# A decoding kernel on one core: TensorE tasks of one column width kept together

## The chip, the core and the metric

The kernel runs on one core of a Trainium2 chip. The core has a matrix engine (TensorE, PE in the profile; its weight loads are PEld), three engines for elementwise work (VectorE or DVE, ScalarE or ACT, GpSimd or POOL) and SyncE (SP), which starts the transfers from main memory. Each engine runs its own instructions in the order in which they were written, and waits on semaphores for the others. TensorE's results go to PSUM, eight banks of 128 partitions by 512 words; everything else lies in SBUF.

TensorE is 128 columns wide. A matmul whose stationary operand has 32 columns or fewer can be placed on one quarter of the array (`tile_position`), one with 64 on one half; up to four or two such matmuls over different columns can then be in the array together. In this text a task is 1-wide, 2-wide or 4-wide when its matmuls use 128, 64 or 32 columns.

The metric is the device time of one execution in microseconds.

## The reference

Eight sequences (B) each decode one token, with x of 448 elements. Two rounds of an attention layer and a dense layer, both with a layer norm in front and the input added behind:

```python
x = x + A(layernorm(x)); x = x + B(layernorm(x)); x = x + A(layernorm(x)); x = x + B(layernorm(x))

def A(x):                        # 16 query heads, 8 key/value heads, head size 256
    q = x @ wq                   # 448 -> 4096
    k, v = the last 1024 positions of the caches, each head used by two query heads
    p = softmax(q k^T / 16)
    return (p v) @ wo            # 4096 -> 448

def B(x):
    return silu(x @ w1) @ w2     # 448 -> 1792 -> 448
```

Both attention layers read the same caches: per sequence eight key and eight value blocks of 512 KB each, 8.4 MB. All is bfloat16, sums are float32.

## The kernel before

**Tiling.** 448 is three chunks of 128 and one of 64, and this last chunk makes for special cases all over the kernel. The weights wq, wo, w1 and w2 stay in SBUF; keys and values pass through 28 slots of 512 KB. A slot is loaded again when its last reader is done, in the fixed order K(0), V(0), K(1), V(1), and so on; SyncE issues these transfers in that order. Keys are transposed within their slot on VectorE (`KT`, L973), sixteen transposes a sequence.

**Stages of a sequence b.** `layer1(b)`: scores of layer 1 (L656, 4-wide) against the transposed keys; softmax (`softmax`, L666 to L702: maximum on VectorE, exponentials on ScalarE, 64-wide transposes of the probabilities at L685, the sum at L696); values (`pv_rows`, 4-wide L715, and `pv_cols`, 1-wide L741); the output projection wo, partly as rows (`rows_part`, 4-wide, L758, into bank XB) and for the last four blocks as columns (`cols_part`, L764, into bank YB). `fold` copies the rows to SBUF (`rowb`, L775) and adds them to the columns with four matmuls (L776). `layer2(b)` then starts with `chain(b)`: `up` evacuates x (`xb_evac`, L784), computes its statistics (`stat`, L789 to L793, then ScalarE and a Newton iteration), multiplies by w1 (L542), and makes hT from tanh (L819), `zh` (L820) and their product (L822); then w2 as rows (8 blocks) and columns (6 blocks, L764), `fold`, `xb_evac` again, the centred copy `xc` (L832 to L836) that ScalarE spreads into `xn`, the second wq (L854), and with it scores, softmax and values of layer 2.

In `cols_part` the four output chunks of a block follow one another: three of 128 columns and the last, 64 wide:

```python
bank[YB][0:(P if o < 3 else 64), o * XW:(o + 1) * XW], lhs(o, i)[:, 0:(P if o < 3 else 64)],
```

**Order of the work.** Sequences don't depend on each other, so layer 1 of the next one runs among layer 2 of this one. No loop sets this order: `add` collects tasks with the tiles that they read and write, and `Plan.schedule` (L79) plays the kernel through with estimated durations. A task's rank is the longest chain of estimated durations behind it. At each step the engine that is free first takes, among the tasks that are ready within 0.2 us, the one of highest rank; where that one isn't ready yet, a task that fits ahead of it. The result is one fixed order per engine; `emit` adds the semaphores.

**Zero matmuls.** Where TensorE would be idle in this plan, `schedule` puts in matmuls of 256 columns with a zero stationary operand (L1020), 128 wide, which add nothing to the bank that they write. It counts the columns streamed in the last 3.41 us and adds zero matmuls while the count is under 4500. A task's `shape` holds the columns that each of its matmuls streams and the number of matmuls that run side by side (1, 2 or 4); the estimated duration comes from it too. Before the change the second number is used for that and for nothing else, and the transposes of the probabilities, 64 wide, carry a 1.

## Time and profile before

| | |
|---|---|
| median of 3 timed runs | 299.21 us (298.16 to 305.74) |
| the profiled execution | 295.94 us, its span 294.2 us |
| mean granted TensorE clock | 0.930 |
| busy: TensorE, its weight loads, VectorE, ScalarE, GpSimd | 83%, 55%, 52%, 25%, 8% |
| transfers | 78.40 MB, mean 267 GB/s over the span |
| chain that ended last | PE 75%, DVE 10%, ACT 6%, DMA 4%, issue 3% |

The span runs from the first to the last instruction of the profiled execution. Busy time of TensorE is the union of its matmuls' times; they are pipelined, so a row such as "1.22 PE L764 ... x16" spans sixteen overlapping matmuls, and the start of the next row tells better how long they kept the engine. A row of grouped instructions reads: line, engine, operation, tile written and tiles read, shape (rows*columns of the stationary operand, then the moving one), count | busy us, mean ns of one | idle us of the engine before them and what ended it. The granted clock is the share of TensorE's full clock that the chip allowed.

### The profile page before, as it was taken

What the parts mean: (1) busy time and instruction counts of PE and PEld (TensorE: products, weight loads), DVE (VectorE), ACT (ScalarE), POOL (GpSimd) and SP (SyncE); (2) the same over time, 40 slices, a digit from 0 to 9 for tenths busy, and PEclk for the clock granted to TensorE, in tenths of its full rate; (3) what the DMA queues carried; (4) which work ended last, traced back from release to release, by engine and by line L of the source; (5) the groups of instructions that cost most, each with busy time, mean ns of one, the idle gap of its engine ahead of it and who ended that gap; (6) DMA issues with size and microseconds to landing.
All of it is one profiled execution on the core that took longest, in us unless ns stands there. A gap on an engine that the chain in (4) does not pass through costs nothing.

```text
span 294.2 us, 11387 instructions
## 1 busy us (share of the span) xinstructions
PE 244.7 (83%) x5159; PEld 161.7 (55%) x5159; DVE 152.7 (52%) x444; ACT 73.0 (25%) x234; POOL 22.7 (8%) x116
## 2 busy tenths in 40 slices
PE   1155659997989889969997999699969997999996
PEld 0142335754566557645664576456635664676863
DVE  7197101379165828660777186536662756122351
ACT  2022301201422062232222422422132221231221
POOL 6000000020002000200020002000200020002000
PEclk9999997989997999995999799989797979997998
DMA  7999999999595598868886987799569876100000
GB/s 266 358 416 406 400 388 347 415 407 410 222 344 219 179 392 285 295 228 345 281 299 214 359 290 287 285 358 316 192 223 370 296 264 218 72 2 4 3 4 1
DMA packets 30880, 78.40 MB, mean 267 GB/s; under 512 B 2272, under 2 KB 5296, under 8 KB 30448
## 3 DMA queue, kind: packets, MB, share of 16 engines
q1 hardware_dynamic: 30832, 77.68, 71.4%
q8 instruction: 40, 0.66, 0.8%
q14 instruction: 8, 0.07, 0.1%
HBM read 77.67 MB, written 0.01 MB: 264 GB/s over the span
## 4 chain that ended last, share of the span: by engine, by line
PE 75%; DVE 10%; ACT 6%; DMA 4%; issue 3%; SPq 1%; ACTq 0%
PE bank L715 14%; PE bank L656 11%; PE bank L1020 8%; PE bank L764 8%; PE bank L542 7%; PE bank L854 7%; PE bank L758 7%; DVE slot L973 6%; DMA slot<-in_A_k_cache_dram 4%; ACT qbd L640 3%; PE bank L685 3%; ACT e_sb L679 2%; PE bank L865 2%; PE bank L696 2%; PE bank L741 1%
## 5 line engine op out<-in xcount | busy, mean ns | idle before, releaser
L973 DVE STREAM_TRANSPOSE slot<-slot 128x512 uint32<-128x512 uint32 x128 | 83.0, 684 | 6.5 <-DMA slot<-in_A_k_cache_dram 6.2
L656 PE MATMUL bank<-slot,qbd 128*8 128x256 bf16 x1024 | 40.3, 292 | 11.7 <-DVE mseg L662 9.8
L715 PE MATMUL bank<-slot,pT_sb 128*2 128x256 bf16 x960 | 43.7, 312 | 0.4 <-ACT pT_sb L693 0.4
L1020 PE MATMUL bank<-wq_sb,cols_b 128*128 128x256 bf16 x218 | 39.0, 292 | 0.3 <-issue 0.3
L656 PEld LDWEIGHTS bank<-slot,qbd 128*8 128x8 bf16 x1024 | 23.2, 87 | 20.3 <-DVE mseg L662 12.8
L715 PEld LDWEIGHTS bank<-slot,pT_sb 128*2 128x2 bf16 x960 | 22.1, 91 | 9.4 <-issue 1.0
L640 ACT ACTIVATE qbd<-q1s 32x128 bf16<-32x128 bf16 x32 | 10.0, 313 | 60.9 <-PE bank L656 60.3
L701 DVE RECIPROCAL rl_sb<-bank 128x16 f32<-128x16 f32 x16 | 4.1, 258 | 40.0 <-PE bank L696 39.7
L1020 PEld LDWEIGHTS bank<-wq_sb,cols_b 128*128 128x128 bf16 x218 | 19.3, 101 | 9.8 <-issue 7.1
L854 PE MATMUL bank<-wq_sb,xn 128*4 128x256 bf16 (+1 forms) x384 | 23.0, 375 | 0.2 <-DVE qT L859 0.2
L726 DVE TENSOR_TENSOR oT<-bank,rl_sb 128x16 bf16<-128x16 f32 (+1 forms) x32 | 6.2, 195 | 32.3 <-PE bank L722 32.2
L720 ACT ACTIVATE o_sb<-bank 128x256 bf16<-128x256 f32 x32 | 12.2, 383 | 34.2 <-PE bank L715 18.7
L820 POOL TENSOR_SCALAR zh<-vt,rstd 128x14 f32<-128x14 f32 x9 | 3.1, 347 | 214.6 <-DVE rstd L561 150.0
L685 PE MATMUL bank<-ident,e_sb 128*64 128x16 bf16 x256 | 9.8, 185 | 11.7 <-ACT e_sb L679 11.4
L758 PE MATMUL bank<-w2o,oT 128*1 128x448 bf16 x256 | 16.8, 376 | 3.1 <-issue 3.1
L859 DVE STREAM_TRANSPOSE qT<-bank 128x256 f32<-128x256 f32 (+1 forms) x24 | 12.1, 525 | 13.1 <-PE bank L854 12.9
L542 PE MATMUL bank<-xbt,w_sb 128*128 128x32 bf16 x504 | 16.0, 177 | 1.7 <-issue 1.4
L685 PEld LDWEIGHTS bank<-ident,e_sb 128*64 128x64 bf16 x256 | 6.9, 116 | 17.8 <-ACT e_sb L679 15.2
L542 PEld LDWEIGHTS bank<-xbt,w_sb 128*128 128x128 bf16 x504 | 14.1, 97 | 3.3 <-issue 1.6
L775 ACT ACTIVATE rowb<-bank 128x448 bf16<-128x448 f32 x17 | 9.2, 543 | 26.6 <-PE bank L758 26.5
L662 DVE TENSOR_REDUCE mseg<-bank 128x1 f32<-128x256 f32 x32 | 12.8, 410 | 5.1 <-PE bank L656 4.8
L764 PE MATMUL bank<-hT,w2o 128*128 128x16 bf16 x192 | 14.7, 180 | 0.6 <-issue 0.6
(161 smaller groups left out, 277.6 us busy)
## 6 DMA issues: line engine op xcount, KB each, us to landing
slot<-in_A_k_cache_dram SPq DMA_DIRECT2D x64, 512.0 KB, 8.0
slot<-in_A_v_cache_dram SPq DMA_DIRECT2D x64, 512.0 KB, 6.1
w2o<-in_A_wo_dram SPq DMA_DIRECT2D x2, 1792.0 KB, 16.1
wq_sb<-in_A_wq_dram SPq DMA_DIRECT2D x3, 1024.0 KB, 6.8
w2o<-in_B_w_dram SPq DMA_DIRECT2D x1, 1568.0 KB, 14.7
w_sb<-in_B_w_dram SPq DMA_DIRECT2D x3, 448.0 KB, 12.0
wq_sb<-in_A_wq_dram SPq DMA_DIRECT2D x2, 256.0 KB, 10.0
w_sb<-in_B_w_dram SPq DMA_DIRECT2D x1, 128.0 KB, 11.7
```

Of the source, the lines that this page charges most:

```text
L542: fns.append(lambda e, o=o, i=i, c0=c0: e.matmul(bank[bank_i][:, c0:c0 + n], lhs(o, i), rhs(o, i).broadcast_to([P, n]) if wide else rhs(o, i),
L640: act(lambda e, q=q: e.activation(qbd[0][32 * q:32 * q + 32].rearrange("p k c (q r) -> p (k c) q r", r=2)[:, :, q, :], q1s[32 * t:32 * t + ...
L656: fns.append(lambda e, cb=cb, par=par, j=j, kvh=kvh, kv=kv: e.matmul(bank[sc][32 * j:32 * j + 8, k2 * 256:(k2 + 1) * 256], qbd[layer][:, k ...
L662: dve(lambda e: e.tensor_reduce(mseg[layer][:, k2:k2 + 1], bank[sc][:, k2 * 256:(k2 + 1) * 256], AX.X, ALU.max, negate=True), bk(sc), [("m ...
L685: pe([lambda e, uh=uh, ql=ql, k2=k2: e.matmul(bank[lb][64 * ql:64 * ql + 64, (k2 * 4 + uh) * 16:(k2 * 4 + uh) * 16 + 16], e_sb[ei][:, k2, ...
L715: fns.append(lambda e, qh=qh, uh=uh, j=j, vv=vv: e.matmul(bank[ob][32 * j:32 * j + 2, c0:c0 + DH], p_col(ei, k2, j, qh, uh), vv, start=(qh ...
L720: act(lambda e: e.activation(o_sb[oi][:], bank[ob][:, c0:c0 + DH], ACTF.Copy), bk(ob), [("o", oi)], 0.385, "oevh" if ob == OB[0] else "oev ...
L758: pe([lambda e, i=i, c=c: e.matmul(bank[XB][32 * c:32 * c + 1, 0:D], rhs(i), w_sb[:, i * D:(i + 1) * D], start=(first and i - i0 < 4), sto ...
L764: pe([lambda e, i=i, o=o: e.matmul(bank[YB][0:(P if o < 3 else 64), o * XW:(o + 1) * XW], lhs(o, i)[:, 0:(P if o < 3 else 64)], rhs(i).bro ...
L854: fns.append(lambda e, j=j, c=c, wb=wb, off=off, h0=h0, n=n, k2=k2: e.matmul(bank[wb][32 * j:32 * j + 4, h0:h0 + n], xn[:, part(c, k2), j, :],
L973: dve(lambda e, v=v: e.transpose(v, v), [("slot", s)], [("slot", s)], 0.67, "KT")
L1020: fill = (lambda e: e.matmul(bank[OB[0]][:, DH:2 * DH], zero_b.broadcast_to([P, P]), wq_sb[:, 0:DH], start=False, stop=True, skip_group_ch ...
```

## The change

Six things change together:

- `cols_part` makes its fourth output chunk 128 wide, like the others. The upper 64 partitions of that chunk then hold products with columns that belong to the next block of the weights. So `xb_evac` takes two copies instead of one: the first three chunks as before, and the fourth with a scale per partition (`mask4`) that is zero in the upper half. The centred copy `xc` is five 1-wide matmuls of 64 columns instead of nine, and ScalarE spreads it into `xn` with three copies instead of two, none of which reads another's result.
- The planner knows a current width (`mode`). A TensorE task of another width starts 0.1 us later (`SWITCH`), and a ready task of the current width gets 0.3 added to its rank (`stay`). Only tasks of the current width are put ahead of one that isn't ready.
- Zero matmuls take the width of the task that follows: one of 128 columns, or two of 64, or four of 32, each 256 streamed columns, planned as 0.107 us in each case. The transposes of the probabilities now count as 2-wide.
- In `up` the statistics go to bank YB and w1 to bank XB, the other way round than before, and w1 is five tasks that go through the inputs chunk by chunk instead of four that go through the outputs. `stat` and `xc` tell the planner their streamed columns (16 and 64 instead of 1 and 4).
- `zh` moves from GpSimd to VectorE. The small transposed maxima `mT` get a tile for each layer.
- Some estimated durations change (second exponential, `va`, `qT`).

```diff
-            best = max(soon, key=lambda t: t.rank)
+            key = (lambda t: t.rank + (stay if t.shape[1] == mode else 0.0)) if e == "pe" else (lambda t: t.rank)
+            best = max(soon, key=key)
...
-                fits = [t for t in soon if ready[t.idx] <= now and now + t.dur <= ready[best.idx] + 0.03]
+                fits = [t for t in soon if ready[t.idx] <= now and now + t.dur <= ready[best.idx] + 0.03
+                        and (e != "pe" or t.shape[1] == mode)]
...
-            best.start = max(free[e], ready[best.idx])
+            best.start = max(free[e] + (SWITCH if e == "pe" and best.shape[1] != mode else 0.0), ready[best.idx])
...
-                        t = Task("pe", [fn], dur, 0.0, "fill")
-                        t.shape = (cols, 1)
+                        t = Task("pe", fns, dur, 0.0, "fill")
+                        t.shape = (cols, best.shape[1])
...
-               [("e", ei, k2), "ident"], bk(lb), (16, 1), "pT%d" % layer)
+               [("e", ei, k2), "ident"], bk(lb), (16, 2), "pT%d" % layer)
...
-            bank[YB][0:(P if o < 3 else 64), o * XW:(o + 1) * XW], lhs(o, i)[:, 0:(P if o < 3 else 64)],
-            rhs(i).broadcast_to([P, XW]), start=False, stop=True, skip_group_check=True)
-            for i in ins for o in range(KC)], reads, bk(YB), (XW, 1), name)
+            bank[YB][:, o * XW:(o + 1) * XW], lhs(o, i), rhs(i).broadcast_to([P, XW]), start=False, stop=True,
+            skip_group_check=True) for i in ins for o in range(KC)], reads, bk(YB), (XW, 1), name)
...
-        act(lambda e: e.activation(xbt[:, 0:KC], xcols(), ACTF.Copy), bk(YB), ["xbt"], 0.18, "xbt")
+        act(lambda e: e.activation(xbt[:, 0:3], xcols()[:, 0:3], ACTF.Copy), bk(YB), [("xbt", 0)], 0.175, "xbt")
+        act(lambda e: e.activation(xbt[:, 3:4], xcols()[:, 3:4], ACTF.Copy, scale=mask4[:, 3:4]), bk(YB) + MASK4,
+            [("xbt", 1)], 0.175, "xbt")
...
-        stat(XB, 0, 4.0, 0)
-        for o0, o1 in ((0, 4), (4, 8), (8, 11), (11, 14)):
-            pe(proj(YB, C_W1 + o0 * CW, range(o0, o1), range(KC), w1_l,
+        stat(YB, C_S1, 4.0, 0)
+        for i, o0, o1 in ((0, 0, FC), (1, 0, FC), (2, 0, FC), (3, 0, 8), (3, 8, FC)):
+            k = i if o0 == 0 else KC
+            pe([lambda e, i=i, k=k, o=o: e.matmul(
+                bank[XB][:, C_W1 + o * CW:C_W1 + o * CW + CW], w1_l(o, i), xbt[:, k:k + 1].broadcast_to([P, CW]),
...
-        pool(lambda e: e.tensor_scalar(zh[:], vt[:], rstds[0][:, 0:1], None, op0=ALU.mult), ["vt", ("rstd", 0)],
-             ["zh"], 0.22, "zh")
+        dve(lambda e: e.tensor_scalar(zh[:], vt[:], rstds[0][:, 0:1], None, op0=ALU.mult), ["vt", ("rstd", 0)],
+            ["zh"], 0.234, "zh")
...
-           [lambda e, c=c: e.matmul(xc[:, 0:3 * XW], ones_b[:], xbt[:, c:c + 1].broadcast_to([P, 3 * XW]),
-                                    start=False, stop=(c == KC - 1), skip_group_check=True) for c in range(KC)] +
-           [lambda e, c=c: e.matmul(xc[0:64, 3 * XW:], ones_b[:, 0:64], xbt[:, c:c + 1].broadcast_to([P, XW]),
+           [lambda e, c=c: e.matmul(xc, ones_b[:], xbt[:, c:c + 1].broadcast_to([P, KC * XW]),
...
-        act(lambda e: e.activation(xd[:, 0:KC], xc[:, 0:KC * XW:XW].unsqueeze(2).broadcast_to([P, KC, 4]), ACTF.Copy,
-                                   scale=-1.0 / D), bk(XB), ["xn"], 0.19, "xn")
-        act(lambda e: e.activation(xd[64:128, 4], xd[0:64, 3], ACTF.Copy), ["xn"], ["xn4"], 0.2, "x4")
+        xv = xc[:, 0:KC * XW:XW].unsqueeze(2).broadcast_to([P, KC, 4])
+        act(lambda e: e.activation(xd[:, 0:3], xv[:, 0:3], ACTF.Copy, scale=-1.0 / D), bk(XB), [("xn", 0)], 0.21, "xn")
+        act(lambda e: e.activation(xd[0:64, 3], xv[0:64, 3], ACTF.Copy, scale=-1.0 / D), bk(XB), [("xn", 1)], 0.19, "xn")
+        act(lambda e: e.activation(xd[64:128, 4], xv[0:64, 3], ACTF.Copy, scale=-1.0 / D), bk(XB), [("xn", 2)], 0.19,
+            "xn")
...
+    fills = {n: [lambda e, j=j, m=P // n: e.matmul(
+        bank[OB[0]][m * j:m * j + m, DH:2 * DH], zero_b.broadcast_to([P, m]), wq_sb[:, 0:DH], start=False, stop=True,
+        skip_group_check=True, **({"tile_position": (0, m * j)} if m < P else {})) for j in range(n)] for n in (1, 2, 4)}
+    fill = (fills, 0.107, DH,
```

## The prediction, made before the change was run

> **What bounds the kernel now.** I read the page from the top, then the chain of work that ended last, then one period of the loop in the timeline.

> ```profile
> span 294.2 us, 11387 instructions
> PE 244.7 (83%) x5159; PEld 161.7 (55%) x5159; DVE 152.7 (52%) x444; ACT 73.0 (25%) x234; POOL 22.7 (8%) x116
> ...
> DMA  7999999999595598868886987799569876100000
> ...
> PE 75%; DVE 10%; ACT 6%; DMA 4%; issue 3%; SPq 1%; ACTq 0%
> ```

> The last row, the chain's shares by engine, says that the end is set by TensorE for three quarters of the time; the other engines appear on it with 10% or less. So a nanosecond of TensorE time counts if it lies on that chain, and not otherwise. The DMA row (tenths, 40 slices of 7.4 us) is full only in the slices from 7 to 74 us, where the weights and the first two batches are loaded. The chain, in order of time, has these pieces in one period of the loop:

> ```profile
> 228.88 1.08 PE bank L764 x16
> ...
> 235.23 1.75 PE bank L764 x24
> ```

> L764 is `cols_part`: 16 matmuls for wo and 24 for w2. All of them stand on the chain. Now the same kind of work in the timeline, one period earlier; the first number is the start, so the distance between two rows is what a group occupied:

> ```profile
> 170.86 1.22 PE L764 MATMUL bank<-oT,w2o 128*128 128x16 bf16 x16
> 172.01 0.61 PE L715 MATMUL bank<-slot,pT_sb 128*2 128x256 bf16 x16
> 172.55 0.57 PE L542 MATMUL bank<-xbt,w_sb 128*128 128x32 bf16 x16
> 172.97 0.24 PE L789 MATMUL bank<-xbt,ones_b 128*128 128x16 bf16 x4
> ...
> 174.81 0.71 PE L1020 MATMUL bank<-wq_sb,cols_b 128*128 128x256 bf16 x5
> 175.35 0.20 PE L722 MATMUL bank<-ident,o_sb 128*128 128x8 bf16 x2
> ...
> 176.53 1.82 PE L764 MATMUL bank<-hT,w2o 128*128 128x16 bf16 x24
> 178.28 0.21 PE L722 MATMUL bank<-ident,o_sb 128*128 128x8 bf16 x2
> ```

> Sixteen w1 matmuls, all 128 columns wide, took 172.97 - 172.55 = 0.42 us, 0.026 each. Sixteen matmuls of `cols_part` took 172.01 - 170.86 = 1.15 us, and 24 took 178.28 - 176.53 = 1.75 us: 0.072 each, though each streams half as many columns. What differs is that every fourth has 64 output columns:

> ```profile
> L764 PE MATMUL bank<-hT,w2o 128*128 128x16 bf16 x144 | 11.2, 174 | 0.0
> L764 PE MATMUL bank<-hT,w2o 128*64 128x16 bf16 x48 | 9.5, 197 | 0.6 <-issue 0.6
> ```

> A round of four costs 0.29 us instead of 0.105, so going to the 64-wide block and back costs 0.18 us, 0.09 for each change of width. The four-wide rows say the same: the 16 matmuls of 256 columns from 172.01 stream in four rounds of 0.108 (five zero matmuls of 256 columns: 0.54 us from 174.81), 0.43 in all, and the next group starts after 0.54. So a change costs about 0.1 us wherever it stands.

> The period itself:

> ```profile
> 104.09:131.05 26.96, 24.43 (x560) 16.47 (x560) 17.11 (x48) 8.71 (x28) 2.10 (x10) 1.00 0.80 294
> 131.05:160.83 29.78, 27.08 (x558) 17.30 (x558) 17.20 (x47) 7.98 (x27) 2.11 (x10) 0.89 0.79 283
> 160.83:188.96 28.13, 25.59 (x560) 16.86 (x560) 17.12 (x48) 8.70 (x29) 2.10 (x10) 0.94 0.83 301
> 188.96:218.66 29.70, 26.90 (x558) 16.94 (x558) 17.14 (x47) 7.98 (x26) 2.11 (x10) 0.89 0.76 276
> 218.66:248.59 29.93, 27.25 (x560) 17.36 (x560) 17.08 (x48) 7.46 (x24) 2.11 (x10) 0.89 0.79 287
> ```

> Columns: stretch, its length, busy time of PE, PEld, DVE, ACT, POOL, then the granted clock, the DMA share and GB/s. Nearly the same work takes 26.96 us at clock 1.00, 28.13 at 0.94 and about 29.8 at 0.89. The clock falls in steps:

> ```profile
> 204.32:207.73 3.41, 2.80 (x52) 2.15 (x52) 1.48 (x4) 0.62 (x3) 0.00 (x0) 1.00 1.00 336
> 207.73:211.14 3.41, 3.41 (x65) 2.02 (x65) 2.32 (x6) 0.85 (x4) 1.44 (x8) 0.50 0.66 246
> ```

> A stretch of 3.41 us with 52 matmuls, most of them the narrow ones of `cols_part`, is followed by one at half clock. One such stretch is 3.41 x 0.5 / 28.1 = 0.06 of a period's clock, so the periods hold zero, one and two of them: each costs (29.8 - 26.96) / 2 = 1.4 us.

> **The change part by part.**

> *No 64-wide blocks in `cols_part`.* Nothing is added on TensorE: the fourth block becomes 128 wide and streams the same 16 columns. The wo part falls from 1.15 to 16 x 0.026 = 0.42 us, a gain of 0.73; the w2 part from 1.75 to 0.63, a gain of 1.12. The latter is capped by what is late next, the row evacuation that the fold waits for:

> ```profile
> 176.64 0.54 ACT L775 ACTIVATE rowb<-bank 128x448 bf16<-128x448 f32 x1 [0.67 <-PE bank L758]
> ...
> 178.35 0.24 PE L776 MATMUL bank<-cols_b,rowb 128*128 128x16 bf16 x4
> 178.63 0.17 ACT L784 ACTIVATE xbt<-bank 128x4 bf16<-128x4 f32 x1 [1.44 <-PE bank L776]
> 179.07 0.20 PE L832 MATMUL bank<-xbt,nident 128*128 128x64 bf16 x1
> 179.52 0.26 PE L789 MATMUL bank<-xbt,ones_b 128*128 128x16 bf16 x4
> ```

> rowb ends at 177.18, so the fold can start near 177.35 instead of 178.35: 1.0 us. Eight times 1.0 and seven of 0.73 (the first batch, at 44 to 58 us, runs in the slices that loading fills, so I count only its w2 part): **13.1 us**.

> *The centred copy (`xc`).* Nine matmuls with a 64-wide group took 179.52 - 179.07 = 0.45 us; five full ones at 0.03 take 0.15: -0.3. Ahead of them the second, masked xbt copy is added. No such copy stands in the trace; the nearest row is the plain one, 0.17, and between 0 (it ends at 178.97, before the 179.07 at which `xc` started because scores of the other layer were on TensorE) and 0.2 with that cover gone. I take 0.1: -0.2 x 8 = **1.6 us**. The third xn copy lies behind the first, which alone the first wq matmuls need: 0.

> *From w1 to hT.* The w1 tasks now go input by input, so only the last 14 of 56 need the masked copy and its 64-row shift; both are done before. The statistics move to the other bank; same matmuls, same dependences. What sets hT:

> ```profile
> 174.94 0.31 ACT L819 ACTIVATE th<-vt,rstd 128x14 f32<-128x14 f32 x1 [0.93 <-DVE rstd L561]
> 175.01 0.35 POOL L820 TENSOR_SCALAR zh<-vt,rstd 128x14 f32<-128x14 f32 x1 [20.27 <-DVE rstd L561]
> 175.17 0.65 DVE L973 STREAM_TRANSPOSE slot<-slot 128x512 uint32<-128x512 uint32 x1
> 175.75 0.13 DVE L822 SCALAR_TENSOR_TENSOR hT<-th,zh 128x14 bf16<-128x14 f32 x1
> ```

> tanh ends at 175.25, zh on GpSimd at 175.36, and hT starts at 175.75 because a transpose of the keys was put on VectorE in between. With zh on VectorE (nearest rows here 0.13 for the same 14 columns and 0.35 on GpSimd; I take 0.2), hT can start about 0.1 after tanh, 0.4 earlier, if no transpose is put there again. Against it the statistics wait for the second copy, 0.17 at most. Between -0.2 and +0.4; I take 0.3: 8 x 0.3 = **2.4 us**. TensorE filled this wait with zero matmuls, so what shrinks is filler.

> The second mT tile takes away an order between two softmaxes that no row shows as a wait: 0.

> *Width changes in the order.* From the first to the last of these rows the timeline of TensorE has 57 changes of width, 20 of them into and out of the 64-wide blocks of L764, two around the one in `xc`, and eight around the transposes of the probabilities, where a 128-wide zero matmul stands between two 64-wide tasks:

> ```profile
> 161.44 0.29 PE L685 MATMUL bank<-ident,e_sb 128*64 128x16 bf16 x8 [1.35 <-ACT e_sb L679]
> 161.67 0.50 PE L1020 MATMUL bank<-wq_sb,cols_b 128*128 128x256 bf16 x3
> ...
> 187.49 0.50 PE L1020 MATMUL bank<-wq_sb,cols_b 128*128 128x256 bf16 x3
> ```

> Those eight stand in waits for the exponentials and gain little. Of the other 27 the planner can merge some; none is 0, all are 2.7 us. A preference of 0.3 in rank can also hold back a task that is due, by one group of the other width (0.1 to 0.5). I take six merged, half of them on the chain: 8 x 0.3 = **2.4 us**.

> *The clock.* The mean clock of 0.930 (cores' table) over 294.2 us makes 0.07 x 294.2 / 1.71 = 12 such stretches.

> ```profile
> 57.55:60.96 3.41, 3.41 (x48) 1.78 (x47) 1.03 (x3) 0.85 (x4) 1.64 (x9) 0.50 1.04 424
> 265.76:269.17 3.41, 3.41 (x58) 1.74 (x58) 0.90 (x2) 0.43 (x2) 1.86 (x10) 0.50 0.00 0
> ```

> Five of them, from this first to this last (with those from 91.68, 207.73 and 238.45), come right behind the w2 part of a batch, as 204.32 to 207.73 showed it. There over a microsecond of near-empty streaming goes and denser work moves in, so I take these five as gone: 5 x 1.4 = **7.0 us**; the ends are 0 and all twelve. The others follow the softmax, where TensorE waits, the start and the tail. [...]

> Sum: 13.1 + 1.6 + 2.4 + 2.4 + 7.0 = 26.5 us. The profiled execution took 295.94 us, its span of 294.2 and 1.7 around it: 269.4. The median of the timed runs, 299.21, lies 3.3 us above it: **273 us**. Per period that is 28.9 - 3.3 = 25.6 us.

> **The rivals.**

> *The clock keeps its steps.* Denser stretches meet the same waits at the softmax, which follow half of the steps, and as many half-clock stretches fall elsewhere in a shorter period. Then 26.5 - 7.0 = 19.5 us are left: 295.94 - 19.5 + 3.3 = 280. Where the small terms (1.6, 2.4, 2.4) end in other waits too, because the planner orders everything anew, 13.1 are left: 286. For it: the steps at 163 and 191 us follow softmaxes alone, and one period had none without any change. Against it: the near-empty stretch that goes is the longest after the softmax. [...]

> *Value transfers arrive last.* DMA is busy for 0.80 x 26.96 = 21.6 to 0.79 x 29.78 = 23.5 us a period, so it is no floor at 25.6. But the second half of the values can be asked for only when the scores have read the keys:

> ```profile
> 184.30 1.91 SPq L514 DMA_DIRECT2D slot<-in_A_v_cache_dram  x4
> 193.77 1.61 PE L715 MATMUL bank<-slot,pT_sb 128*2 128x256 bf16 x40
> slot<-in_A_v_cache_dram SPq DMA_DIRECT2D x64, 512.0 KB, 6.1
> ```

> Issued until 186.2, landed 6.1 later (192.3), first needed at 193.77: 1.5 us of slack. What this change saves lies mostly behind that point. If transfers, closer packed, land 3 us later than now, 1.5 us after their use, a period keeps 1.8 of 3.3 us: 295.94 - 8 x 1.8 + 3.3 = 285.

> *Slower: narrow zero matmuls that don't run side by side.* A zero matmul of 0.107 becomes two or four over a half or a quarter of the columns. The planner still counts 0.107. Were four of them to run one after another, each would take 4 x 0.108 = 0.43, 0.32 too much, at the worst place: right ahead of scores, values and w2 rows. The page has 218 zero matmuls; from 26.5 / 0.32 = 83 of them four-wide on the chain the gain is gone, and with all 218 it would be 273 + 70 = 343. Against it: 16 four-wide matmuls of the same 256 columns took four rounds above.

> *It doesn't do what it says.* The cost might come from the slices that the fourth block loads, not from its width; then a full-width block loads more and the time stays near 299. Against it: the other width changes cost the same 0.1.

> **How the numbers follow.** Forecast, 263 to 278: 0.57. The clock keeps its steps, 278 to 288: 0.26. Late values, about 285: 0.06. It does nothing, 294 to 303: 0.05. Slower by the zero matmuls or an order that the preference spoils, above 305: 0.06. The range 263 to 288 leaves out the last two and the tails of the others, under 0.2; its low end is the sum with all twelve half-clock stretches gone (7 x 1.4 = 9.8 lower). Two per cent, what a measurement of this kernel tells from no change, is 293 to 305: faster 0.90, same 0.05, slower 0.05.

> **What would show it.** Rows of L764 (or its new line) with one form, 128*128, at 0.026 to 0.03 from start to start; no 64-wide row but the transposes of the probabilities and the two-wide zero matmuls; a clock above 0.93 and periods of 25 to 26 us; hT within 0.2 us of tanh's end. The prediction is wrong if these groups shrink and the fold or xbt still comes as late, by a wait for rowb, for hT, or for values, or if the zero matmuls of four take over 0.2 us a set.

## The result and the profile after

The changed kernel took 282.03 us (median of four runs, 280.74 to 283.53), the kernel before 298.69 beside it (295.07 to 305.74): a ratio of 0.948, 95% interval 0.938 to 0.959. It is faster by 16.7 us. Forecast were 273 us and a gain of 26.5, so 10 us are missing; 280 and 286 were the values of the first rival, the clock that keeps its steps. The profiled execution took 282.27 us, 13.7 less than the one before.

Executions of one program differ in time and in clock (experiment 2's four runs: 275.73 us at a mean clock of 0.944 to 290.56 at 0.882), so times are given as medians of all runs, and ratios are taken between undisturbed ones, those within 1.5% of the fastest of their kernel.

The page of the changed kernel: its span, busy times, the queue that the page calls instruction (q8), and the chain that ended last.

```profile
span 280.5 us, 11813 instructions
...
PE 224.1 (80%) x5360; PEld 147.1 (52%) x5360; DVE 154.1 (55%) x453; ACT 74.8 (27%) x259; POOL 19.5 (7%) x107
...
q8 instruction: 42, 0.69, 0.9%
...
PE 65%; DMA 12%; DVE 10%; issue 6%; ACT 5%; SPq 2%; ACTq 0%
```

TensorE gave up 20.6 us of busy time and ten points of the chain. They went to DMA (4% to 12%) and to issue, time in which an engine waited for nothing that the profile shows (3% to 6%: 9.4 us before, 16.7 now). So only part of what TensorE saved reached the end.

Where in the run? Both traces cut at the first wo row of the first and of the last sequence: start, seven periods, tail. Columns: stretch, its length, busy time of PE, PEld, DVE, ACT, POOL, then granted clock, DMA share, GB/s. Before:

```profile
0.00:44.42 44.42, 18.38 (x359) 12.77 (x360) 20.96 (x62) 7.41 (x19) 5.44 (x34) 0.99 0.98 373
44.42:253.78 209.36, 189.03 (x3944) 123.45 (x3948) 119.49 (x326) 56.28 (x183) 14.75 (x70) 0.92 0.80 295
253.78:294.16 40.38, 37.34 (x864) 25.50 (x852) 12.26 (x56) 9.32 (x33) 2.56 (x12) 0.92 0.01 3
```

After:

```profile
0.00:44.65 44.65, 19.17 (x414) 13.28 (x415) 21.00 (x62) 7.41 (x19) 5.44 (x34) 1.00 0.98 371
44.65:237.56 192.91, 165.28 (x4031) 107.28 (x4031) 119.14 (x327) 56.16 (x200) 12.25 (x63) 0.92 0.88 320
237.56:280.49 42.93, 39.68 (x921) 26.52 (x917) 13.98 (x64) 11.26 (x40) 1.86 (x10) 0.80 0.01 3
```

The seven periods lost 16.5 us, 2.35 each where 3.3 were forecast, at the same clock of 0.92. The tail got 2.55 us longer in this profile, and its clock fell from 0.92 to 0.80.

The places that the prediction worked on, in one period of the changed kernel (timeline of TensorE; L770 is `cols_part`, L764 `rows_part`, L781 the fold, L845 and L847 `xc`):

```profile
134.27 0.55 PE L770 MATMUL bank<-oT,w2o 128*128 128x16 bf16 x16
134.75 0.39 PE L721 MATMUL bank<-slot,pT_sb 128*2 128x256 bf16 x8
...
138.64 0.55 PE L764 MATMUL bank<-w2o,hT 128*1 128x448 bf16 x8
139.12 0.76 PE L770 MATMUL bank<-hT,w2o 128*128 128x16 bf16 x24
139.74 0.19 PE L728 MATMUL bank<-ident,o_sb 128*128 128x8 bf16 x2
139.84 0.26 PE L781 MATMUL bank<-cols_b,rowb 128*128 128x16 bf16 x4
...
140.52 0.20 PE L845 MATMUL bank<-xbt,nident 128*128 128x64 bf16 x1
140.56 0.29 PE L847 MATMUL bank<-xbt,ones_b 128*128 128x64 bf16 x4
140.69 0.25 PE L798 MATMUL bank<-xbt,ones_b 128*128 128x16 bf16 x4
```

The wo part now occupies 134.75 - 134.27 = 0.48 us (1.15 before), the w2 part 139.74 - 139.12 = 0.62 (1.75), and from the first w2 row to the fold pass 1.20 us (176.04 to 178.35, 2.31, before). Five `xc` matmuls take 0.17 (0.45). All L770 rows have one form:

```profile
L770 PE MATMUL bank<-hT,w2o 128*128 128x16 bf16 x192 | 6.1, 170 | 0.0
L770 PE MATMUL bank<-oT,w2o 128*128 128x16 bf16 x128 | 4.4, 170 | 0.0
```

The other engines at the same place:

```profile
137.91 0.31 ACT L832 ACTIVATE th<-vt,rstd 128x14 f32<-128x14 f32 x1 [1.42 <-DVE rstd L567]
137.91 0.24 DVE L833 TENSOR_SCALAR zh<-vt,rstd 128x14 f32<-128x14 f32 x1
...
138.36 0.11 DVE L835 SCALAR_TENSOR_TENSOR hT<-th,zh 128x14 bf16<-128x14 f32 x1
...
140.14 0.17 ACT L791 ACTIVATE xbt<-bank 128x3 bf16<-128x3 f32 x1 [0.35 <-PE bank L781]
140.21 0.26 ACT L792 ACTIVATE xbt<-bank,mask 128x1 bf16<-128x1 f32 x1
```

hT starts 0.14 us after the end of tanh (138.22), where it was 0.50; over the eight sequences the mean fell from 0.43 to 0.06. The masked copy overlaps the plain one and ends 0.16 later.

What took the gain back stands in the waits: who waited for what, us in total, times, longest. Before, TensorE after its start:

```profile
PE bank L542 <- issue: 1.4, 2, 0.8
PE bank L764 <- issue: 0.6, 1, 0.6
```

After:

```profile
PE bank L764 <- issue: 4.2, 3, 2.2
...
PE bank L662 <- issue: 3.1, 4, 2.0
...
PE bank L721 <- DMA slot<-in_A_v_cache_dram: 2.9, 3, 1.6
...
PE bank L721 <- issue: 2.2, 3, 1.3
...
PE bank L1033 <- issue: 1.9, 2, 1.0
```

The longest wait of L764 (2.2 us) lies in the start. The gaps over 0.3 us behind the first wo row make 10.3 us in 12 gaps after, 2.0 in 3 before. Value transfers, never waited for before, are waited for three times, 2.9 us. The longest gap but the start's:

```profile
164.35 0.75 PE L662 MATMUL bank<-slot,qbd 128*8 128x256 bf16 x19
167.09 0.39 PE L662 MATMUL bank<-slot,qbd 128*8 128x256 bf16 x5 [1.98 <-issue]
```

TensorE stops in the middle of one task's scores, whose operands are all there. What falls together with the stop is a transfer of the instruction queue, here in the window from 164.5 to 165.7:

```profile
q1 hardware_dynamic: 117, 0.41, 86.1%
q8 instruction: 1, 0.02, 5.1%
```

q8 carried 0.69 MB in 42 packets, 16 KB each, against 40 packets before. This one ran from 164.68 to 165.66 beside the cache transfers (q1), and TensorE went on 2.4 us after its start. The same holds for the other gaps: 2.2 to 2.6 us from the start of a q8 packet to the next matmul. I call them waits for instructions; the profile itself names no cause, and the places are what I infer it from. Numbered through the program, the matmuls at which TensorE goes on stand a whole number of steps of 127.4 matmuls apart (here 600, 727, 1109, 1492, ... 4167), and so do all 128 such gaps of the fourteen traces, on one common grid, within 3.2 matmuls (my count). The packets give nearly the same number: 5360 matmuls came with 42 packets, 127.6 each. Most packet borders are passed without such a stop: 12 of 39 behind the first wo row stopped this run.

### The profile page after: what moved, and what is told of

Its sections match the earlier page's. It is cut to its first block, busy times and chain, and to the rows that moved or that the text cites. A ratio compares the mean times of both kernels' runs of the same rounds, so it can differ in the third digit from the quotient of the medians.

```text
span 280.5 us, 11813 instructions
## 1 busy us (share of the span) xinstructions
PE 224.1 (80%) x5360; PEld 147.1 (52%) x5360; DVE 154.1 (55%) x453; ACT 74.8 (27%) x259; POOL 19.5 (7%) x107
## 4 chain that ended last, share of the span: by engine, by line
PE 65%; DMA 12%; DVE 10%; issue 6%; ACT 5%; SPq 2%; ACTq 0%
PE bank L721 14%; PE bank L662 9%; DMA slot<-in_A_v_cache_dram 8%; PE bank L764 8%; PE bank L1033 6%; DVE slot L986 6%; PE bank L867 6%; PE bank L823 5%; DMA slot<-in_A_k_cache_dram 4%; PE bank L770 3%; PE bank L548 3%; PE bank L691 2%; ACT qbd L646 2%; PE bank L878 2%; PE bank L702 1%
## 5 line engine op out<-in xcount | busy, mean ns | idle before, releaser
L721 PE MATMUL bank<-slot,pT_sb 128*2 128x256 bf16 x960 | 46.4, 315 | 5.4 <-DMA slot<-in_A_v_cache_dram 2.9
L662 PE MATMUL bank<-slot,qbd 128*8 128x256 bf16 x1024 | 38.9, 288 | 10.7 <-DVE mseg L668 4.2
L1033 PE MATMUL bank<-wq_sb,cols_b 128*32 128x256 bf16 (+2 forms) x451 | 34.1, 308 | 1.9 <-issue 1.9
L662 PEld LDWEIGHTS bank<-slot,qbd 128*8 128x8 bf16 x1024 | 24.1, 86 | 20.6 <-DVE mseg L668 5.3
L1033 PEld LDWEIGHTS bank<-wq_sb,cols_b 128*32 128x32 bf16 (+2 forms) x451 | 17.5, 108 | 9.5 <-issue 7.2
L867 PE MATMUL bank<-wq_sb,xn 128*4 128x256 bf16 (+1 forms) x384 | 19.9, 330 | 0.3
L764 PE MATMUL bank<-w2o,oT 128*1 128x448 bf16 x256 | 17.5, 383 | 2.6 <-issue 2.6
L668 DVE TENSOR_REDUCE mseg<-bank 128x1 f32<-128x256 f32 x32 | 13.2, 415 | 10.8 <-PE bank L662 10.3
L556 POOL TENSOR_SCALAR rstd<-va 128x1 int32<-128x1 int32 x8 | 1.5, 190 | 226.6 <-ACT va L813 226.6
L691 PEld LDWEIGHTS bank<-ident,e_sb 128*64 128x64 bf16 x256 | 7.2, 118 | 14.3 <-ACT e_sb L685 12.6
L872 DVE STREAM_TRANSPOSE qT<-bank 128x256 f32<-128x256 f32 (+1 forms) x24 | 11.8, 516 | 5.2 <-PE bank L867 5.2
L685 ACT ACTIVATE e_sb<-bank,mb,rstd 128x256 bf16<-128x256 f32 x16 | 8.6, 564 | 7.4 <-DVE mb L681 7.3
## 6 DMA issues: line engine op xcount, KB each, us to landing
slot<-in_A_k_cache_dram SPq DMA_DIRECT2D x64, 512.0 KB, 8.4
slot<-in_A_v_cache_dram SPq DMA_DIRECT2D x64, 512.0 KB, 6.6
wq_sb<-in_A_wq_dram SPq DMA_DIRECT2D x2, 256.0 KB, 10.3
```

The source lines that it names most:

```text
L662: fns.append(lambda e, cb=cb, par=par, j=j, kvh=kvh, kv=kv: e.matmul(bank[sc][32 * j:32 * j + 8, k2 * 256:(k2 + 1) * 256], qbd[layer][:, k ...
L668: dve(lambda e: e.tensor_reduce(mseg[layer][:, k2:k2 + 1], bank[sc][:, k2 * 256:(k2 + 1) * 256], AX.X, ALU.max, negate=True), bk(sc), [("m ...
L691: pe([lambda e, uh=uh, ql=ql, k2=k2: e.matmul(bank[lb][64 * ql:64 * ql + 64, (k2 * 4 + uh) * 16:(k2 * 4 + uh) * 16 + 16], e_sb[ei][:, k2, ...
L721: fns.append(lambda e, qh=qh, uh=uh, j=j, vv=vv: e.matmul(bank[ob][32 * j:32 * j + 2, c0:c0 + DH], p_col(ei, k2, j, qh, uh), vv, start=(qh ...
L764: pe([lambda e, i=i, c=c: e.matmul(bank[XB][32 * c:32 * c + 1, 0:D], rhs(i), w_sb[:, i * D:(i + 1) * D], start=(first and i - i0 < 4), sto ...
L867: fns.append(lambda e, j=j, c=c, wb=wb, off=off, h0=h0, n=n, k2=k2: e.matmul(bank[wb][32 * j:32 * j + 4, h0:h0 + n], xn[:, part(c, k2), j, :],
```

## The experiments

**1. The blocks alone.** The kernel before with the fourth chunk 128 wide, the masked copy, the five `xc` matmuls and three `xn` copies; the planner, its 128-wide zero matmuls, w1 and `zh` as before.

```diff
-            bank[YB][0:(P if o < 3 else 64), o * XW:(o + 1) * XW], lhs(o, i)[:, 0:(P if o < 3 else 64)],
+            bank[YB][:, o * XW:(o + 1) * XW], lhs(o, i),
...
```

> The kernel before, with only the blocks changed: the fourth chunk of cols_part 128 wide, the masked copy, the five-matmul xc and the three xn copies; planner, zero matmuls, banks and zh as before. My theory (the blocks pay 0.18 us each, wherever they stand): 13 to 15 us below before, 284 to 287, L764 at 0.026 to 0.03 us a matmul. If in addition the half-clock stretches behind the w2 part go: 277 to 281 and a clock of 0.95 or more. Rival (most of the gain of the whole change came from the planner's width rule): 292 to 299.

284.87 us (279.79 to 290.59), the kernel before beside it 297.89: -13.0. The ratio, 0.956, says the same. The wo part takes 0.48 us here and the w2 part 0.61, as in the changed kernel. Nearly all of the gain is in this part. The page's chain:

```profile
PE 70%; DVE 12%; ACT 7%; issue 6%; DMA 4%; SPq 1%; ACTq 0%
```

Issue is at 6% already here, 8 gaps of 9.1 us behind the first wo row, and DMA still at 4%. So waits for instructions come with the shorter blocks already, and those for values with the rest. The clock did rise here, from a mean of 0.922 (the 13 runs of the kernel before beside it) to 0.938 (four runs).

**2. All zero matmuls 128 wide.** The changed kernel's order, each set of zero matmuls one of 128 columns again: fewer instructions, and 43 more width changes.

```diff
-    fills = {n: [... for j in range(n)] for n in (1, 2, 4)}
+    fills = {n: [lambda e: e.matmul(bank[OB[0]][:, DH:2 * DH], zero_b.broadcast_to([P, P]), wq_sb[:, 0:DH], ...)]
+             for n in (1, 2, 4)}
```

> The changed kernel with the same order of work, but every zero matmul is one of 128 columns again, also where the planner meant two of 64 or four of 32. Theory A (the new idle times of TensorE put down to issue, about 8 us against 2 before, come from the sets of four, which bring eight instructions in 0.1 us): these gaps fall to 3 us or less, the time to 275 to 280 in spite of the width changes that come back around the zero matmuls. Rival B (any denser order of TensorE runs out of instructions): the gaps stay at 6 us or more and the time is 282 to 288.

280.32 us (275.73 to 290.56), ratio 0.928 (0.921 to 0.936). This ratio, like that of experiment 4, was taken against the first seven of the thirteen runs of the kernel before; against all thirteen it is 0.940. Either way the kernel is no slower than the changed one, in spite of 241 width changes against 198 (counted over the trace). The waits for instructions didn't shrink with the instructions (40 q8 packets): 10 gaps, 12.6 us. So the narrow zero matmuls are not what makes these gaps (theory A falls, though the time is below what rival B had), and their width gains nothing that can be measured. Values are waited for longer than in the changed kernel (4.6 us against 2.9):

```profile
PE bank L721 <- DMA slot<-in_A_v_cache_dram: 4.6, 3, 2.1
```

That four narrow zero matmuls run side by side is seen in the changed kernel:

```profile
178.91 0.62 PE L1033 MATMUL bank<-wq_sb,cols_b 128*32 128x256 bf16 x16
179.44 0.83 PE L721 MATMUL bank<-slot,pT_sb 128*2 128x256 bf16 x24
```

Four sets in 0.53 us, with a change of width in front of them. Those of 64 columns run in pairs: the sixteen from 71.25 us of that trace started two at a time (within 4 ns), a pair every 0.11 to 0.13 us.

**3. The blocks back.** The changed kernel with the fourth chunk 64 wide again.

```diff
-            bank[YB][:, o * XW:(o + 1) * XW], lhs(o, i), rhs(i).broadcast_to([P, XW]), start=False, stop=True,
+            bank[YB][0:(P if o < 3 else 64), o * XW:(o + 1) * XW], lhs(o, i)[:, 0:(P if o < 3 else 64)],
+            rhs(i).broadcast_to([P, XW]), start=False, stop=True,
```

> The changed kernel with the fourth chunk of cols_part 64 wide again, all else as changed. Theory (0.18 us for each of the 80 blocks, 72 to 80 of them on the path): 13 us above the changed kernel, 293 to 297. Rival (in the new order the waits for values and for instructions end last and hide part of it): 284 to 290.

296.01 us (289.44 to 300.99), ratio 0.991 (0.972 to 1.009): no difference from the kernel before, and above the changed one by 14.0 us by the medians, 11 to 13 by the ratios (0.991 against 0.948 and, in experiment 5, 0.952). With experiment 1 the blocks' worth is shown from both sides, 11 to 14 us. Everything else in the change is 2 us by these medians and isn't told from nothing. Waits for instructions are longer than in the kernel before here too, 6.2 us in 8 gaps, so the blocks are not their only source.

**4. Lighter values.** The changed kernel, but from the second sequence on the transfers of the last four heads' values bring half of their bytes. The other half is left out, so the attention is computed with what the slot held.

```diff
+        m = 512 if b and kvh >= 4 else 1024
-        dma(lambda e: e.dma_start(slots[s][:, :].rearrange("p (h n) -> p h n", h=2),
+        dma(lambda e: e.dma_start(slots[s][:, :].rearrange("p (h n) -> p h n", h=2)[:, :, 0:m],
...
```

> The changed kernel, same order, but from the second sequence on the last four value blocks of a sequence bring only half their bytes (the other half of the slot keeps what stood there, so the computed values differ). Theory C (values landing late cost the changed kernel): no idle time of TensorE that ends on a value transfer, chain share of DMA 5% or less instead of 12%, 2.9 us of idle time gone and with it up to two half-clock stretches: 275 to 280. Rival (something else is as late as the values): 281 to 283.

276.52 us (273.03 to 284.12), ratio 0.926 (0.918 to 0.935); against all thirteen runs of the kernel before it is 0.937, where the changed kernel has 0.948 and 0.952. No wait of TensorE for values is left. The chain:

```profile
PE 64%; SPq 13%; DVE 7%; ACT 6%; issue 5%; DMA 4%; ACTq 0%
```

DMA is back at 4%. Lighter transfers save 5.5 to 7 us by the medians (282.03 and 283.54 against 276.52) and 3 to 4.5 by these ratios. That late values are the reason isn't shown. Experiment 2 comes out about as low (0.940) with 4.6 us of waits for values, and experiment 6 has no such wait and the changed kernel's time. Whether less traffic brought instructions and keys earlier too, no reading here shows.

**5. The changed kernel once more**, beside experiments 6 to 8 on one chip; nothing is edited.

> The changed kernel itself, unaltered, beside the next ones on one chip: 280 to 284, and the ratio to before between 0.94 and 0.96.

283.54 us (282.15 to 288.70), ratio 0.952 (0.948 to 0.957). Two of the rows behind a wait for instructions:

```profile
169.82 0.39 PE L662 MATMUL bank<-slot,qbd 128*8 128x256 bf16 x5 [3.57 <-issue]
225.44 0.91 PE L764 MATMUL bank<-w2o,hT 128*1 128x448 bf16 x6 [1.98 <-issue]
```

It stopped at the same matmul as before (five scores left of the same task, six w2 rows left of the same task), with other lengths. The place belongs to the program, not to chance. The clock of the tail doesn't: the same instructions, profiled again, ran there at 0.92 instead of 0.80, in 40.88 us instead of 42.93.

```profile
239.82:280.70 40.88, 36.70 (x921) 25.21 (x917) 13.78 (x64) 11.08 (x40) 1.87 (x10) 0.92 0.04 15
```

Stretches of the clock don't begin with the kernel: behind 40 us the first half-clock stretch starts at 43.89 us in the trace of before and at 45.85 in that of after, about 3.0 and 1.5 us past a whole number of stretches of 3.41. I take it that two executions of one kernel cut the same stream at other points in the same way; that isn't shown. A tail's clock in one profile is one draw: the six traces of the changed kernel's order with these matmuls (after, experiments 2, 3, 4, 5 and 8) have 5, 2, 7, 5, 2 and 5 half-clock stretches there.

**6. No width rule.** The changed kernel with a planner that doesn't see widths: no 0.1 us per change, no preference, and tasks of any width are put ahead.

```diff
-SWITCH = 0.1
+SWITCH = 0.0
...
-    def schedule(self, ..., stay=0.3):
+    def schedule(self, ..., stay=0.0):
...
-                        and (e != "pe" or t.shape[1] == mode)]
```

> The changed kernel, but the planner orders as before: no 0.1 us for a change of width, no 0.3 in rank for staying, no width condition for tasks put ahead. If the planner's rule is worth what the prediction gave it (0.3 us a period): 2 to 3 us above the changed kernel, with 10 to 20 more changes of width a period. If orders of fewer changes only pack the same waits (values, instructions): within 1.5 us of it. If holding on to a width makes weak stretches and late tasks: below it.

284.76 us (279.04 to 288.51), ratio 0.943 (0.936 to 0.949): no difference from the changed kernel beside it. The rule avoids 10 width changes (208 without it, 198 with it, 269 in experiment 1, 462 before; counted over the trace). Against that stand two losses. One is the second wq. Two rows of one sequence without the rule, of which the second waits for the last wq part:

```profile
150.15 0.47 PE L877 MATMUL bank<-qT,irep 128*128 128x64 f32 x2
...
152.43 0.47 PE L877 MATMUL bank<-qT,irep 128*128 128x64 f32 x2
```

With the rule:

```profile
143.10 0.45 PE L878 MATMUL bank<-qT,irep 128*128 128x64 f32 x2
143.48 0.82 PE L867 MATMUL bank<-wq_sb,xn 128*4 128x512 bf16 x12
144.13 1.12 PE L662 MATMUL bank<-slot,qbd 128*8 128x256 bf16 x32
145.04 0.42 PE L867 MATMUL bank<-wq_sb,xn 128*4 128x512 bf16 x4
...
146.39 0.47 PE L878 MATMUL bank<-qT,irep 128*128 128x64 f32 x2 [0.72 <-DVE qT L872]
```

32 scores of the other layer, 4-wide as wq is, go ahead of wq's last four matmuls, and the next step comes after 3.29 us instead of 2.28. Five of the eight sequences lose 0.5 to 1.0 us so. Whether this reaches the end isn't shown. The other loss is the clock. Without the rule its mean is 0.943 over the six runs, 0.915 in experiment 5, and in the profile the tail holds no half-clock stretch:

```profile
241.76:279.25 37.49, 34.19 (x912) 24.31 (x900) 13.97 (x64) 10.76 (x40) 1.87 (x10) 1.00 0.01 3
```

With the rule it was 0.80 and 0.92. What can happen there the changed kernel's own windows show:

```profile
254.06:257.47 3.41, 3.41 (x126) 3.05 (x125) 1.86 (x7) 0.00 (x0) 0.00 (x0) 1.00 0.02 5
257.47:260.88 3.41, 3.41 (x88) 2.68 (x89) 0.57 (x3) 1.72 (x5) 0.00 (x0) 0.50 0.02 5
```

In the first stretch TensorE was busy without a break, and half clock followed. Most of its 126 matmuls are the last wo's, which stream 7 columns each and follow one another in long groups (80 in a row). In all the stretch streamed 2,685 columns (my count, two or four side by side counted once; at the 0.108 us of a zero matmul of 256 columns a full stretch would hold some 8,100).

**7. More zero matmuls.** The planner's target raised from 4500 to 9000 streamed columns in 3.41 us.

```diff
-    def schedule(self, ..., target=4500.0, first=40.0, stay=0.3):
+    def schedule(self, ..., target=9000.0, first=40.0, stay=0.3):
```

> The changed kernel, with zero matmuls in every wait that the planner sees (9000 columns in 3.41 us asked for instead of 4500). If a half-clock stretch costs 1.4 us: a mean clock of 0.97 or more and 273 to 277. If the waits for values and instructions make the weak stretches, where the plan has no room for zero matmuls: a clock of 0.91 to 0.95 and 279 to 284.

293.06 us (287.69 to 295.61), ratio 0.978 (0.970 to 0.985), 9.5 slower than the changed kernel beside it, which neither expectation had. The mean clock rose to 0.934 (0.915 in experiment 5, both over the six runs), but 935 zero matmuls in place of 451 delay what comes behind them and bring more waits for instructions: 15 gaps of 19.5 us, 46 q8 packets. So more filler raises the clock a little, and the time with it.

**8. Shifted instructions.** 64 matmuls of 8 columns at the start, so that all later instructions lie elsewhere in their 16 KB packets.

```diff
+        pe([lambda e: e.matmul(bank[LB[0]][:, 0:8], ident[:], ident[:, 0:8], start=True, stop=True)] * 64, ["ident"],
+           bk(LB[0]), (8, 1), "shift")
```

> The changed kernel, with 64 small matmuls (128 TensorE instructions) more in the wait for wq at the start, so that all later TensorE instructions stand half a fetch of 16 KB further on. If the idle times put down to issue are waits for the next 16 KB of instructions: they end at other places of the work than in the changed kernel (there before the scores at 167, w2 rows at 222, values at 156), none longer than 2.5 us after the start, and the time moves by up to 4 us either way. If they belong to the work at these places: the same lines in the same sequences, and the time within 1 us.

282.10 us (279.05 to 285.85), ratio 0.945 (0.939 to 0.950). All gaps moved. The two places of experiment 5 run through here, and others break; two of them, lines counted two higher:

```profile
162.65 0.27 PE L723 MATMUL bank<-slot,pT_sb 128*2 128x256 bf16 x2 [1.48 <-issue]
...
185.64 2.50 PE L723 MATMUL bank<-slot,pT_sb 128*2 128x256 bf16 x45 [2.03 <-issue]
```

So a gap's place follows from where an instruction lies in the stream, not from the work it does. The sum (13.2 us in 10 gaps) and the time stayed: nothing is won by moving them. What the program would take without them no run shows.

**9. More columns in the tail.** The last wo, w1 and w2 stream each of their seven columns four times; every fourth result is read. The order is the changed kernel's.

```diff
+        G = 4
+        n4 = G * nb
-                    lambda o, i: oT2[:, i % 2, i // 2, 0:nb], nb, fresh=False),
+                    lambda o, i: oT2[:, i % 2, i // 2, 0:nb].unsqueeze(2).broadcast_to([P, nb, G]), n4, fresh=False),
...
-        xp = bank[xa][:, 0:KC * nb].rearrange("p (c b) -> p c b", b=nb)
+        xp = bank[xa][:, 0:KC * n4:G].rearrange("p (c b) -> p c b", b=nb)
...
```

> The changed kernel, and in the last sequence's closing work for seven sequences at once (final_rows) each matmul streams 28 columns, every value four times, instead of 7; same number of matmuls, same result. If the half-clock stretches of the tail (five in one execution of the changed kernel, two in another, none where the width rule was left out) come from matmuls of 7 columns that occupy TensorE and stream little: the tail at clock 0.95 or more, 2 to 6 us below the changed kernel, 277 to 281. If the clock goes by busy time: nothing changes, 281 to 285.

279.07 us (276.72 to 280.24), ratio 0.942 (0.933 to 0.951). The tail, from its window:

```profile
238.77:278.26 39.49, 36.19 (x921) 24.86 (x917) 13.80 (x64) 11.06 (x40) 1.85 (x10) 0.95 0.03 7
```

The same 921 matmuls, at a clock of 0.95 instead of 0.80 and 0.92, 3.4 and 1.4 us less. One half-clock stretch is left in this tail; the six traces with 7 columns had 2 to 7, and experiments 11 and 12 with 28 columns none. (Other orders do with 7 columns too: experiment 6 has none, experiment 10 two.) Only the streamed columns differ, and they cost little. The mean clock of the six runs is 0.935, that of experiment 5 was 0.915. The last wo in the changed kernel:

```profile
L548 PE MATMUL bank<-oT,w2o 128*128 128x7 bf16 x128 | 3.7, 167 | 0.0
```

and here:

```profile
L548 PE MATMUL bank<-oT,w2o 128*128 128x28 bf16 x128 | 3.7, 174 | 0.0
```

This agrees with a clock that is kept by columns streamed, not by the time TensorE is busy. The gain in the whole, 3.0 and 4.5 us by the medians of the changed kernel here and in experiment 5, lies inside the intervals of the ratios, although all six runs (at most 280.24) are below all ten of the changed kernel (at least 280.74).

**10. The penalty without the preference.** `SWITCH` kept, `stay` at zero, tasks of any width put ahead.

```diff
-    def schedule(self, ..., stay=0.3):
+    def schedule(self, ..., stay=0.0):
...
-                        and (e != "pe" or t.shape[1] == mode)]
```

> The changed kernel with the planner counting 0.1 us for a change of width, but without the 0.3 in rank for staying and without the width condition for tasks put ahead. If the preference packs work of one width and few columns together and so costs clock: a mean clock 0.01 to 0.025 above the changed kernel, at about the same time or up to 4 us below it. If the preference is what saves changes of width: 2 to 3 us above it.

280.18 us (277.25 to 286.74), ratio 0.945 (0.935 to 0.955). Scores stand between the wq parts here too (144.92 to 148.23 from one of these rows to the next, 3.31 us), so this loss comes from the 0.1 us in the planner's count, not from the preference. The 0.1 us alone doesn't lower the number of width changes either: 218 by the same count, against 208 without any rule and 198 with both parts. The mean clock is 0.942 in the six runs.

**11 and 12. Combinations.** Experiment 9's tail with the planner of 6, and with that of 10.

> The order without the width rule together with the wider streams of the tail. The tail of that order ran at full clock already, so by the theory of columns this adds 0 to 2 us to it: 279 to 284, equal to the order without the rule.

> The changed kernel without the preference for staying (0.1 us for a change of width still counted) and with the wider streams in the closing work. By the theory both gains came from the clock, of different places (loop and tail), so they add in part: a clock of 0.945 to 0.965 and 276 to 279, ratio to before 0.92 to 0.935. If the two are one and the same gain: 279 to 281.

282.94 us (279.71 to 284.29), ratio 0.953 (0.942 to 0.965), and 281.34 (275.94 to 283.36; before beside it 298.44). The mean clock of the first rose to 0.96, and the time didn't follow: the gains don't add; the second lies above both of its expectations. None of these versions stands clear of the changed kernel; the lowest median among them is experiment 9's.

## Why the prediction was right, and where it was wrong

The time lies in the stated range of 263 to 288 us, but not in its likelier part, 263 to 278; it lies where the first rival had it. That it is near the rival's 280 is in part luck: this number kept 6.4 us of small terms, of which the runs show little in the end, and knew nothing of waits for instructions. The rival's other value, 286 with the blocks alone, is not much further off. Of the signs that the prediction named, the one form of L764 and hT came, the clock above 0.93 and periods of 25 to 26 us didn't (0.915, and 27.6 in the mean).

- **No 64-wide blocks, 13.1 us: right.** Per sequence 0.67 (forecast 0.73) and, up to the fold, 1.11 (1.0); in the run 11 to 14 lost when taken back, and 13.0 won by it and the next term alone (14.7 forecast). The price of 0.09 to 0.1 us for a change of width holds. The rival that loads are what costs falls: with more columns to load, a round takes 0.10 us.
- **`xc`, 1.6 us: right in size.** -0.28 (-0.3) and 0.16 for the masked copy (0.1); xbt's first reader in `stat` starts 0.85 us after the fold starts, 1.17 before.
- **From w1 to hT, 2.4 us: right at its place, not seen in the end.** 0.36 in the period shown, 0.37 in the mean of eight sequences, against 0.3. But what the changed kernel has beyond experiment 1 is 1.3 to 2.8 us by the medians (284.87 against 283.54 and 282.03), 1 to 2 by the ratios (0.956 against 0.952 and 0.948), where this term and the next two made 11.8.
- **Width changes by the planner, 2.4 us: wrong.** The step that failed is "six merged, half of them on the chain": the rule avoids 10 changes in the whole run, and beside them stand 0.5 to 1.0 us in five sequences ahead of the second wq and a lower clock (experiment 6). The prediction had a price for the preference, but none for the 0.1 us counted in the plan, which is what moves the scores.
- **The clock, 7.0 us: wrong.** The step that failed is "I take these five as gone". The profile has 14 half-clock stretches where there were 12 (13 in experiment 5's). With the blocks alone there were 8 in the profile, and none of them right behind a w2 part, so at that place the five did go; two came new behind waits for instructions (201.86 and 222.34 of that trace), which grew from 2.0 to 9.1 us. These are counts of one profile each; by the mean clock of its four runs, 0.938, experiment 1 had about ten. In the changed kernel's periods weak stretches come behind waits for instructions (from 165.3 and 219.9 us) and behind the softmax and the values (from 97 and 203). The prediction counted which thin stretches go, not which come when TensorE waits more. Its own example, the stretch from 204.32, held such a wait of 0.61 us, and 21 of its 52 matmuls were of `cols_part`, not most. Idle time alone doesn't mark them: the stretch from 254.06 was busy for 3.41 of 3.41 us, and half clock followed.
- **Missing altogether: waits for instructions.** The trace of before had them, 2.0 us in three gaps and a q8 row. The prediction read "issue 3%" and went on. On the chain issue went from 9.4 to 16.7 us, 10.2 of it in the twelve gaps. How much of these 7.3 us the end would get back isn't shown.
- **The rivals.** "The clock keeps its steps" came true, in value (280 to 286) and in its mechanism: half-clock stretches fell elsewhere, some of them behind waits that it didn't name. "Value transfers arrive last" came true in part: values are waited for, 2.9 us where its price was 285 - 273 = 12, and what that costs is open (experiment 4). Its slack of 1.5 us was already too wide, since it took the median of 6.1 us to landing: in the trace of before the last of the four transfers was issued at 185.73 and landed at 193.01, 0.76 us before the first use. Zero matmuls side by side: four sets took 0.53 us, so the slower case falls.

By the medians, the missing 10 to 12 us divide so: 1.7 on the blocks with `xc` (14.7 forecast, 13.0 measured), and 9.0 to 10.5 on the other three terms, of which the clock is 7.0 and the merging 2.4. How the latter divide between the clock, the wq order, the late values and the waits for instructions stays open: they overlap, and experiments 10 to 12 show that removing one doesn't shorten the whole by its price.

## What to carry to other kernels

A change of TensorE's column width cost about 0.1 us here where TensorE was what came last, and nothing that could be measured beside zero matmuls (experiment 2: 280.32 us with 43 changes more). So give a narrow rest of a tile the full width if the surplus can be masked by one cheap copy. Before counting what a faster TensorE stream saves, look in the waits for the lines with "issue" and for the slack of the next transfers: here the chain's time in "issue" grew by 7.3 us, and values were waited for 2.9 us. And count streamed columns per stretch when a clock is to be kept: matmuls of 7 columns, most of the stretch from 254.06, kept TensorE busy for 3.41 of 3.41 us with 2,685 columns, and half clock followed all the same.
